# Later casts, products with v in groups of three key tiles, and the weight conversion issued ahead of the silu step

## The chip, the cores and the metric

The kernel runs on one core of a Trainium2 chip. TensorE multiplies matrices, VectorE and ScalarE do elementwise work and reductions, GpSimd (POOL in the profile) does elementwise work and issues the indirect transfers, SyncE (SP) issues the other transfers. Each engine works through its own instructions in order and waits on semaphores for the others. The metric is the device time of one execution in microseconds: 639.28 us for the kernel before, the median of 3 runs (638.69 to 642.12).

## The reference

Three stages, all in float32, on 1536 tokens (batch 2, sequence 768) of 512 features (8 heads of 64):

```python
# 1. attention among the keys whose 6 sign bits are those of the query
mask = q_bucket[:, :, :, None] == k_bucket[:, :, None, :]
scores = np.where(mask, scale * np.matmul(q, k.transpose(0, 1, 3, 2)), -1e9)
attn = softmax(scores)                      # over the 768 keys
x = np.matmul(attn, v)                      # then (tokens, 512)
# 2. dense layer with silu, 512 -> 2048 -> 512
h = x @ w_in
x = (h / (1 + np.exp(-h))) @ w_out
# 3. 8 experts, 512 -> 1024 -> 512; a token takes the expert of its largest logit,
#    and none where its skip score is not positive
y = gate * (np.maximum(xc @ w1[e], 0) @ w2[e])
out[do_compute] = xc + y
```

## The kernel before, in words

**Attention** (function `attention`, L264 to L597). Two heads make a pair; there are eight pairs (i = 0 to 7), and each has two halves of 384 queries, the units u = 0 to 15. A step is one block of 128 queries of one head: six steps per unit (`PU`), twelve per pair, 96 in all (`NS`). In the loop at L535, m is the step within the pair and pm the step within the unit. Step s issues the following, and each engine takes its part in this order:

- `em_S(s)` (L380): TensorE, four products of queries and keys into a PSUM tile S of two banks. There are two such tiles, so step s waits until the exponential of step s-2 has read its own.
- `em_T(s-2, 0)` (L409): TensorE transposes the first three of the six key tiles of P of step s-2 into a tile T (three of them); ScalarE copies them to PT.
- the casts of `PRE` for the next pair, on ScalarE: `kh` (keys) and `qa` (queries), once per head.
- `em_PV` (L426) in every second step: the products with v for two key tiles and two heads. They belong to the unit before. A unit has six key tiles, k = 0 to 5, so three such steps.
- `em_soft(s)` (L394): VectorE's row maximum mx and a small operation bs, then ScalarE's exponential into P.
- `em_T(s-2, 1)`: the other three key tiles; VectorE copies them (in the last pair ScalarE).
- `em_rc` and `em_r` (L434, L438): reciprocals of the row sums on VectorE, a transpose rT on TensorE, a copy r on ScalarE, a transfer to DRAM (r_d), and two transfers back (rb) that wait for the first. `em_out` copies the finished products; `em_x` multiplies and splits them on GpSimd.
- the operations of `POST` for the next pair: `k2` and `qb` are transfers by SP that copy a cast half to the other partitions, `kl` and `ql` are subtractions on GpSimd. Then the mask rows (`prep_rows`), loads, and at the end of the step the hook, which during pairs 2 to 5 and at the end also issues pieces of the first weight conversions.

For pair 0, which prepares pair 1, a second list of `PRE` and `POST` is used, with other step numbers.

**The silu layer** (L600 to L669, loop at L859). There are 3 blocks of 512 tokens and 16 slices f of 128 hidden features, 48 steps n. Products use a float32r high part and a remainder (hi and lo). A step multiplies (`em_h(n)`: 12 matmuls into ph on TensorE; then silu g and its cast gh on ScalarE, and the remainder gl = g - gh on VectorE, L625 to L627), then `em_out(n-1)` does the 12 matmuls o with the step before's gh, gh and gl. In the first block the weights still have to be converted from 64-bit words (`convert`, L197): for f of 4 to 15 step n = f - 2 runs `convert(f)`. Its first part (two ScalarE scalings u, L214, and two VectorE shifts, L215) is issued inside the split of the weights of step n+1 (ScalarE's whi, L249, VectorE's wlo, L252); its second part (two VectorE operations at L219, two at L223 which give wraw, then two loads of later words by SP) is issued by `for _ in cv: pass`. Weights of 512 KB halves are staged in three buffers. In the second and third block the converted weights are used again.

**The experts** follow from L916 on and are not touched.

The lines that the change touches are L528 to L533 (the lists), L551 to L553 (the products with v), L566 (the step in which r is made) and L870 to L874:

```python
if n < N:
    if n >= len(EARLY_H):
        em_h(n)
    for _ in cv:
        pass
```

Of the kernel before, what the change touches and what calls it, by code (L numbers as in the profile page):

```python
# [25 lines left out]
def kernel(  # L26
# [16 lines left out]
    nc = tc.nc  # L43
# [190 lines left out]
    def split(i):  # L234
        assert next(splitting(i), "end") == "end"
# [28 lines left out]
    def attention(hook):  # L264
# [26 lines left out]
        def prep_alloc(i):  # L291
            pl = mainp if i % 2 else evp
            ops[i] = [pl.tile([P, 2, S], F32R, name=n, bufs=1) for n in ("Q1", "K1", "Q2")] + [K2s[i % 2]]
            mks[i] = (topp.tile([P, HQ], F32, name="ma"), topp.tile([P, HQ], F32R, name="mb"))
# [78 lines left out]
        units = [(i, qh) for i in range(B * NP) for qh in range(2)]  # L373
# [6 lines left out]
        def em_S(s, parts=(0, 1)):  # L380
            u, qt, hd = steps[s]
            i, qh = units[u]
            Q1, K1, Q2, K2 = ops[i]
            q0 = qh * HQ + qt * P
            if 0 in parts:
                st_S[s] = psS.tile([P, 2, 512], F32, tag="S", name="S", bufs=2)
            ps = st_S[s]
            for j in parts:
                q_, k_, n, first = ((Q1, K1, P, True), (Q2, K2, NK2, False))[j]
                for c in range(2):  # L390
                    nc.tensor.matmul(ps[:, c, 0:HQ], q_[0:n, hd, q0:q0 + P], k_[0:n, hd, c * HQ:(c + 1) * HQ],  # L391
                                     start=first, stop=not first)
# [33 lines left out]
        def em_PV(u, k):  # L426
            i, qh = units[u]
            if k == 0:
                st_pv[u] = psTV.tile([P, HQ], F32, tag="V", name="pv", bufs=1)
            for hd in range(2):  # L430
                nc.tensor.matmul(st_pv[u][hd * D:(hd + 1) * D], vts[i][:, k, hd], st_PT[u][:, hd, k],  # L431
                                 start=(k == 0), stop=(k == KT - 1))
# [45 lines left out]
        def em_busy(n):  # L478

            for _ in range(n):  # L480
                nc.tensor.matmul(bs, busy[:, 0:P], busy, start=True, stop=True)
# [21 lines left out]
        for j, ps in enumerate(direct):  # L503
# [6 lines left out]
            else:  # L510
# [14 lines left out]
        prep_op(1, 0, "scale", nc.scalar)  # L525
        nc.gpsimd.memset(K2s[1][D:D + 32].bitcast(F32), 0.0)

        PRE = [(1, 0, "kh", nc.scalar), (3, 0, "qa", nc.scalar), (5, 1, "kh", nc.scalar), (7, 1, "qa", nc.scalar)]  # L528

        POST = [(1, 0, "k2", None), (2, 0, "kl", nc.gpsimd), (3, 0, "qb", None), (4, 0, "ql", nc.gpsimd),  # L530
                (5, 1, "k2", None), (7, 1, "kl", nc.gpsimd), (7, 1, "qb", None), (9, 1, "ql", nc.gpsimd)]

        PRE, POST = ([ops_, [(x + 2, *op) for x, *op in ops_]] for ops_ in (PRE, POST))  # L533
        rbs, xs = {}, {}
        for s in range(NS + PU + 4):  # L535
            i, m = divmod(s, 2 * PU)
            nxt = i + 1 < B * NP
            if nxt and m == 0:
                prep_alloc(i + 1)
            if s < NS:  # L540
                em_S(s, (0, 1) if s else (1,))
            if 0 <= s - 2 < NS:
                em_T(s - 2, 0)
            for mm, *op in PRE[i == 0]:
                if nxt and mm == m:
                    prep_op(i + 1, *op)
            w, pm = divmod(s, PU)
            u, k = (w - 1, pm - 2) if pm >= 2 else (w - 2, pm + 4)
            pv = 0 <= u < len(units)

            if pv and k % 2:  # L551
                em_PV(u, k - 1)
                em_PV(u, k)  # L553
            if s < NS:
                em_soft(s)
            if s == 1:
                prep_op(0, 1, "k2", nc.scalar)
                prep_op(0, 1, "kl", nc.vector)
            if s < 2:
                em_busy(2)  # L560
            if 0 <= s - 2 < NS:
                em_T(s - 2, 1)
            if pv:
                if k == 0:
                    em_rc(u)
                if k == 1:  # L566
                    rbs[u] = em_r(u)
                if k == KT - 1:
                    xs[u] = em_out(u)
                if k == 3 and u:  # L570
                    em_x(u - 1, xs.pop(u - 1), rbs.pop(u - 1), nc.gpsimd)
            if nxt:
                if m == (1 if i else 5):
                    prep_proj(i + 1)
                if m == (2 if i else 6):
                    prep_mask(i + 1, nc.gpsimd if i else nc.scalar)
                for mm, *op in POST[i == 0]:
                    if mm == m:
                        prep_op(i + 1, *op)
                if m == (4 if i else 8):  # L580
                    prep_rows(i + 1)
                if m == 0 and i + 2 < B * NP:
                    prep_load(i + 2)
                if m == (9 if i else 11) and i + 2 < B * NP:
                    prep_op(i + 2, 0, "scale", nc.scalar)
                if m == 11 and i + 2 < B * NP:
                    load_v(i + 2)
                if m == 11 and i + 2 == B * NP:
                    top_st.close()
            if s == NS - 2 * PU:  # L590
                ev_st.close()
            hook(s - NS)
            if s == NS - 1:
                psS_st.close()
# [246 lines left out]
    with tc.manual_schedule():  # L841
# [17 lines left out]
        for n in range(N + 1):  # L859
            cv = convert(n + 2) if NEARLY <= n + 2 < NF else iter(())  # L860
            while cnt["spl"] < min(n + (3 if n >= NF else 2), N):

                sp = splitting(cnt["spl"], apart=True)
                next(sp)
                next(cv, None)
                next(sp, None)
            if n >= N - 2:
                while cnt["spl"] < NM + (1 if n == N - 2 else 3) and any(h[1] > 1 for h in homes):
                    split(cnt["spl"])
            if n < N:  # L870
                if n >= len(EARLY_H):
                    em_h(n)
                for _ in cv:
                    pass  # L874
            if n == NF - 2:
                pools["stg_st"].close()
                pools["gwb"], gwb_st = opened("gwb", side="right")
                pools["gwb_t"] = pools["gwb"].tile([P, NE + 1, DM], F32, name="gwb")
                nc.sync.dma_start(pools["gwb_t"].rearrange("p c d -> p (c d)"), gr.to_broadcast([P, (NE + 1) * DM]))
            if n == 3:  # L880
                cf = pools["xo"].tile([P, DM], F32, tag="x", name="cf", bufs=6)
                nc.sync.dma_start(cf[:, 0:consts.shape[1] - NC - P], consts[:, NC + P:])
            if n == 6:
                nc.vector.tensor_copy(cb, cf[:, 0:consts.shape[1] - NC - P])
            if n == 1:
                nc.sync.dma_start(tk, tok)
                nc.gpsimd.memset(gwc, 0.0)
                nc.sync.dma_start(gwc[:, :, 0:NE + 1], gw.rearrange("(k p) c -> p k c", p=P))
                z = pools["gwb0"] = sm.tile([P, NE * NTOK // P], F32, name="zid", bufs=1)
                nc.gpsimd.memset(z, float(DUMMY))  # L890
                nc.sync.dma_start(id_d.rearrange("(p r) c -> p (r c)", p=P), z)
                zx = sm.tile([P, DM // P], F32, name="zx", bufs=1)
                nc.gpsimd.memset(zx, 0.0)
                nc.sync.dma_start(x_d[NTOK:NTOK + 1].rearrange("o (p c) -> (o p) c", p=P), zx)
                nc.sync.dma_start(g_d[NTOK:NTOK + 1], zx[0:1, 0:1])
            if n >= 1:
                em_out(n - 1)
                b, f = items[n - 1]
                if f == NF - 1 and b + 1 < len(TILES):
                    todo.extend((t, c) for t in range(*TILES[b]) for c in range(NE + 1))  # L900
            if routing is not None and next(routing, "end") == "end":
                routing = None
            if n % NF:
                for j in range(4):
                    if todo:
                        logit(*todo.pop(0))
                        if not todo:
                            bb = n // NF - 1
                            if idx is None:
                                idx = ps_tile("idx", [P, 3], "O4")  # L910
                            routing = route(*TILES[bb], L[:, TILES[bb][0]:TILES[bb][1]], ps_tile("pr", [P, 512], "X"), idx)
# [49 lines left out]
        for t in range(t1 - t0):  # L961
            x = pools["xo"].tile([P, DM], F32, tag="x", name="x", bufs=6) if t < 2 else ep.tile([P, DM], F32, tag="eo", name="x")
# [280 lines left out]
```

## Time and profile before

| | |
|---|---|
| runs of the kernel before | 639.28 us median (638.69 to 642.12, n = 3) |
| the profiled execution | 640.85 us, of which the span 639.0 us |
| TensorE matmul busy | 610.4 us (96%) |
| VectorE busy | 468.9 us (73%) |
| ScalarE busy | 403.8 us (63%) |
| GpSimd busy | 171.0 us (27%) |
| chain of waits that ended last | TensorE 74%, ScalarE 9%, VectorE 7%, issue 4%, transfers 3% |

The profile is of one execution. "Busy" counts the time in which an engine executes; matmuls are pipelined, so a busy TensorE is not one at its peak. The chain of waits is followed back from the last instruction, at each step to what released it or to the instruction before it on its engine: what stands in it set the end. Attention takes about the first 235 us, the silu layer goes to about 517, the experts from about 544 to the end.

### The profile page before, as it was taken

The page shows a single profiled execution, that of the slowest core. Times are in us where ns is not written, and L with a number is a line of the kernel's source. Part 1 is how long each engine was busy: PE and PEld are TensorE (multiplying, and loading weights), DVE is VectorE, ACT ScalarE, POOL GpSimd, SP SyncE. Part 2 cuts the span into 40 slices and gives each one's busy share as a digit, 9 for nine tenths or more (in the row PEclk, how much of TensorE's full clock was granted, in tenths as well). Part 3 has the DMA queues.
Part 4 walks back from the last instruction along what each step waited for, and adds up shares of the span by engine and source line. Part 5 has one row for each costly group of instructions (what it writes and reads, how often), then busy time and mean ns, then how long its engine had stood idle before and what let it go on. Part 6 is the DMA issues. An engine that isn't in the chain of part 4 may idle for free.

```text
span 639.0 us, 9525 instructions
## 1 busy us (share of the span) xinstructions
PE 610.4 (96%) x3239; PEld 461.9 (72%) x3239; DVE 468.9 (73%) x861; ACT 403.8 (63%) x675; POOL 171.0 (27%) x261
## 2 busy tenths in 40 slices
PE   8899999999999999998899999999999988999996
PEld 3667676666767756776678888788887766788885
DVE  6867778788787665778776777447775568899992
ACT  6978788787887984454555333444433456788881
POOL 4437556383744142000000000020000035523201
PEclk9999999999999999999999999999999999999998
DMA  3532542534224124545443000007223258999920
GB/s 109 148 120 64 173 108 82 157 74 129 65 57 105 78 78 114 176 162 168 151 146 148 0 1 2 0 3 197 90 80 128 66 132 224 363 406 406 408 78 27
DMA packets 30978, 83.45 MB, mean 131 GB/s; under 512 B 6032, under 2 KB 9810, under 8 KB 30798
## 3 DMA queue, kind: packets, MB, share of 16 engines
q1 hardware_dynamic: 28834, 79.06, 38.5%
q0 software_dynamic: 1936, 3.65, 1.7%
q8 instruction: 26, 0.43, 0.3%
q14 instruction: 26, 0.21, 0.1%
q10 hardware_dynamic: 156, 0.10, 0.1%
HBM read 67.65 MB, written 8.50 MB: 119 GB/s over the span
## 4 chain that ended last, share of the span: by engine, by line
PE 74%; ACT 9%; DVE 7%; issue 4%; DMA 3%; POOL 1%; SPq 1%; POOLq 0%; DVEq 0%; ACTq 0%
PE ph L619 17%; PE o L662 10%; PE S L391 9%; PE pv L431 9%; PE T L417 8%; PE o L653 7%; PE eh L1059 5%; PE ey L1081 5%; ACT P L405 3%; ACT u L214 2%; DVE mag L219 2%; DVE mx L401 1%; PE tr L1037 1%; DVE wraw L223 1%; ACT K L317 1%
## 5 line engine op out<-in xcount | busy, mean ns | idle before, releaser
L249 ACT CAST whi<-wraw 128x1024 fp32r<-128x1024 f32 x100 | 102.7, 1050 | 45.0 <-DVE wraw L223 38.1
L252 DVE TENSOR_TENSOR wlo<-wraw,whi 128x1024 fp32r<-128x1024 f32 x100 | 119.6, 1222 | 11.5 <-ACT whi L249 10.5
L405 ACT ACTIVATE P<-S,bs 128x768 f32<-128x768 f32 x96 | 95.5, 994 | 26.0 <-DVE bs L403 23.2
L401 DVE TENSOR_REDUCE mx<-S 128x1 f32<-128x768 f32 x96 | 91.1, 949 | 14.2 <-PE S L391 11.8
L391 PE MATMUL S<-K,Q 88*128 88x384 f32 (+1 forms) x384 | 92.5, 362 | 7.8 <-ACT P L405 6.0
L625 ACT ACTIVATE g<-ph 128x512 f32<-128x512 f32 x48 | 28.5, 595 | 107.1 <-PE ph L619 93.7
L417 PEld LDWEIGHTS T<-ident,P 128*128 128x128 f32 x576 | 68.0, 140 | 30.9 <-ACT PT L420 18.6
L627 DVE TENSOR_TENSOR gl<-g,gh 128x512 fp32r<-128x512 f32 x48 | 33.3, 693 | 77.0 <-ACT gh L626 77.0
L417 PE MATMUL T<-ident,P 128*128 128x128 f32 x576 | 88.7, 277 | 0.2 <-ACT PT L420 0.2
L791 POOL DMA_INDIRECT id_d<-tk,slot x12 | 12.1, 1006 | 261.6 <-DVE pre L799 258.5
L391 PEld LDWEIGHTS S<-K,Q 88*128 88x128 f32 (+1 forms) x384 | 63.0, 191 | 16.0 <-ACT P L405 8.8
L431 PE MATMUL pv<-PT,v 128*64 128x384 f32 x384 | 72.5, 499 | 0.0
L422 DVE COPY PT<-T 128x384 f32<-128x384 f32 x85 | 47.0, 553 | 22.0 <-PE T L417 21.3
L619 PE MATMUL ph<-xhi,whi 128*128 128x512 f32 x192 | 54.4, 405 | 6.4 <-ACT whi L249 6.4
L420 ACT COPY PT<-T 128x384 f32<-128x384 f32 x107 | 50.6, 479 | 9.4 <-PE T L417 8.7
L619 PE MATMUL ph<-xlo,whi 128*128 128x512 f32 x192 | 52.3, 394 | 0.0
L619 PE MATMUL ph<-xhi,wlo 128*128 128x512 f32 x192 | 52.1, 393 | 0.0
L619 PEld LDWEIGHTS ph<-xhi,whi 128*128 128x128 f32 x192 | 34.6, 188 | 17.8 <-ACT whi L249 10.6
L675 DVE CUSTOM_DVE_ANT_0 junk<-x,gwb 128x512 bf16<-128x512 f32 x72 | 45.4, 686 | 0.0
L619 PEld LDWEIGHTS ph<-xlo,whi 128*128 128x128 f32 x192 | 36.1, 188 | 8.5
L619 PEld LDWEIGHTS ph<-xhi,wlo 128*128 128x128 f32 x192 | 36.1, 188 | 8.3
L431 PEld LDWEIGHTS pv<-PT,v 128*64 128x64 f32 x384 | 23.3, 136 | 25.5 <-issue 25.2
(177 smaller groups left out, 1049.9 us busy)
## 6 DMA issues: line engine op xcount, KB each, us to landing
wraw<-in_w_dram SPq DMA_DIRECT2D x64, 512.0 KB
w<-in_mw_dram SPq DMA_DIRECT2D x32, 512.0 KB
v<-in_vt_dram SPq DMA_DIRECT2D x8, 384.0 KB
rb<-r_d SPq DMA_DIRECT2D x32, 96.0 KB
out_dram<-x SPq DMA_DIRECT2D x12, 256.0 KB
x_d<-x SPq DMA_DIRECT2D x11, 256.0 KB
raw<-in_kT_dram SPq DMA_DIRECT2D x7, 384.0 KB
raw<-in_qT_dram SPq DMA_DIRECT2D x7, 384.0 KB
```

What stands on the lines that cost most here:

```text
L249: nc.scalar.copy(hi[:, sl], t[:, sl])
L252: eng.tensor_tensor(lo[:, sl], t[:, sl], hi[:, sl].bitcast(F32), op=ALU.subtract)
L391: nc.tensor.matmul(ps[:, c, 0:HQ], q_[0:n, hd, q0:q0 + P], k_[0:n, hd, c * HQ:(c + 1) * HQ], start=first, stop=not first)
L401: nc.vector.tensor_reduce(mx[:, 0:1], ps[:, :, 0:HQ], axis=AX.XY, op=ALU.max, negate=True)
L405: nc.scalar.activation(pt.rearrange("p (a b) -> p a b", a=2), ps[:, :, 0:HQ], AF.Exp, bias=bs_[:, 0:1], scale=bs_[:, 1:2], accum_out=st_su ...
L417: nc.tensor.transpose(ps[:, j], pt[:, k * P:(k + 1) * P], ident)
L420: nc.scalar.copy(dst, ps)
L422: nc.vector.tensor_copy(dst, ps)
L431: nc.tensor.matmul(st_pv[u][hd * D:(hd + 1) * D], vts[i][:, k, hd], st_PT[u][:, hd, k], start=(k == 0), stop=(k == KT - 1))
L619: nc.tensor.matmul(p_[:, 0:c1 - c0], w[:, k * P:(k + 1) * P], x[:, k, t0 * P + c0:t0 * P + c1], start=(q == 0), stop=(q == len(ops3) - 1))
L662: nc.tensor.matmul(acc[t], g[:, (t - t0) * P:(t - t0 + 1) * P], w[:, DM:PIECE], start=(f == 0 and q == 0), stop=(f == NF - 1 and q == 2))
L675: nc.vector.tensor_tensor_reduce(junk, xts[t], pools["gwb_t"][:, c], op0=ALU.mult, op1=ALU.add, scale=1.0, scalar=0.0, accum_out=L[:, t, c ...
```

## The change

There are four edits.

1. The casts and copies for head 1 of the next pair are issued in later steps (for pairs 1 and later): casts in 7 and 9 rather than 5 and 7, the transfers k2 and qb in 7 and 9 rather than 5 and 7, the subtractions in 8 and 10 rather than 7 and 9. In pair 0 all of them get other numbers: casts in 2, 4, 6, 8 (before: 3, 5, 7, 9), k2 and qb in 2, 4, 6, 8 (before: 3, 5, 7, 9), kl and ql in 3, 5, 7, 9 (before: 4, 6, 9, 11).
2. The products with v are issued for three key tiles in every third step rather than for two in every second.
3. For the last unit r is made at k = 3 rather than at k = 1.
4. In the silu layer the second part of the conversion is issued before em_h(n) rather than after it.

```diff
-        PRE = [(1, 0, "kh", nc.scalar), (3, 0, "qa", nc.scalar), (5, 1, "kh", nc.scalar), (7, 1, "qa", nc.scalar)]
+        PRE = [(1, 0, "kh", nc.scalar), (3, 0, "qa", nc.scalar), (7, 1, "kh", nc.scalar), (9, 1, "qa", nc.scalar)]
         POST = [(1, 0, "k2", None), (2, 0, "kl", nc.gpsimd), (3, 0, "qb", None), (4, 0, "ql", nc.gpsimd),
-                (5, 1, "k2", None), (7, 1, "kl", nc.gpsimd), (7, 1, "qb", None), (9, 1, "ql", nc.gpsimd)]
-        PRE, POST = ([ops_, [(x + 2, *op) for x, *op in ops_]] for ops_ in (PRE, POST))
+                (7, 1, "k2", None), (8, 1, "kl", nc.gpsimd), (9, 1, "qb", None), (10, 1, "ql", nc.gpsimd)]
+        PRE, POST = ([ops_, [(x + (1 if x < 5 else -1), *op) for x, *op in ops_]] for ops_ in (PRE, POST))
...
-            if pv and k % 2:
+            if pv and k % 3 == 2:
+                em_PV(u, k - 2)
                 em_PV(u, k - 1)
                 em_PV(u, k)
...
-                if k == 1:
+                if k == (1 if u + 1 < len(units) else 3):
                     rbs[u] = em_r(u)
...
             if n < N:
+                for _ in cv:
+                    pass
                 if n >= len(EARLY_H):
                     em_h(n)
-                for _ in cv:
-                    pass
```

## Rows read from the trace of the kernel before

**Rows 1.** Busy time by stretch: PE, PEld, DVE, ACT, POOL, clock, DMA share, GB/s

```profile
270.00:329.70 59.70, 53.38 (x222) 40.58 (x220) 45.46 (x74) 30.65 (x47) 0.00 (x0) 1.00 0.41 135
```

**Rows 2.** Chain of waits (start us, us, what), first block of the silu layer

```profile
284.18 1.24 ACT u L214 x2
...
286.60 0.69 DVE gl L627
...
290.69 1.23 ACT u L214 x2
```

**Rows 3.** Chain of waits, second block of the silu layer

```profile
352.11 2.80 PE ph L619 x12
354.91 2.76 PE o L662 x12
```

**Rows 4.** Timeline (start, us, engine, line, idle before), one step of the first block

```profile
284.31 1.23 DVE L252 TENSOR_TENSOR wlo<-wraw,whi 128x1024 fp32r<-128x1024 f32 x1 [0.22 <-ACT whi L249]
...
287.21 1.29 DVE L219 SCALAR_TENSOR_TENSOR mag<-u,mag 128x512 int32<-128x512 int32 x2
...
288.41 1.29 DVE L223 SCALAR_TENSOR_TENSOR wraw<-u,mag 128x512 int32<-128x512 int32 x2
...
289.62 0.76 DVE L215 TENSOR_SCALAR mag<-w 128x512 int32<-128x512 int32 x2
289.73 1.05 ACT L249 CAST whi<-wraw 128x1024 fp32r<-128x1024 f32 x1 [3.17 <-DVE wraw L223]
```

**Rows 5.** Chain of waits, attention of the last pair of heads

```profile
194.29 1.44 PE pv L431 x8
195.73 0.48 PE T L417 x3
196.21 0.70 PE S L391 x4
196.91 0.66 PE T L417 x6
```

**Rows 6.** Chain of waits, step 3 of pairs 1 and 7, and a projection

```profile
45.90 1.44 PE pv L431 x8
...
69.94 0.78 PE pj L338 x8
...
211.64 1.44 PE pv L431 x8
```

**Rows 7.** Timeline of attention, single instructions

```profile
26.01 0.98 PE L391 MATMUL S<-K,Q 128*128 128x384 f32 x4 [0.78 <-ACT P L405]
...
39.34 0.94 PE L391 MATMUL S<-K,Q 128*128 128x384 f32 x4 [1.47 <-DMA Q<-Q]
...
107.64 0.84 ACT L317 ACTIVATE K<-raw 64x768 fp32r<-64x768 f32 x1
...
117.69 0.24 ACT L444 COPY r<-rT 6x128 f32<-6x128 f32 x1
...
119.20 1.11 SPq L448 DMA_DIRECT2D rb<-r_d  x2
...
239.85 0.27 PE L442 MATMUL rT<-ident,sums 128*6 128x128 f32 x1 [1.00 <-DVE sums L436]
```

**Rows 8.** Chain of waits, from S to the end of its exponential

```profile
226.95 0.72 PE S L391 x4
...
227.69 0.97 DVE mx L401
...
228.68 0.17 DVE bs L403
...
228.94 1.08 ACT P L405 x2
```

**Rows 9.** The page's groups of instructions: ScalarE's copies of transposed tiles

```profile
L420 ACT COPY PT<-T 128x384 f32<-128x384 f32 x107 | 50.6, 479 | 9.4 <-PE T L417 8.7
```

**Rows 10.** Chain of waits, the transfer that copies Q for pair 1

```profile
36.12 3.08 DMA Q<-Q
```

## The prediction

> **What bounds the kernel now.** I cut the span into stretches first. From 270 to 329.7 us TensorE is busy for 53.4 of 59.7 us, at the full clock [rows 1]: something else paces it there. The chain of waits of that stretch repeats the same pieces every 6.51 us (ScalarE's u at 284.18 and 290.69), and between them stands VectorE's gl [rows 2]. Further on, a step of the silu layer is only its twelve ph and twelve o matmuls, 2.80 + 2.76 = 5.56 us [rows 3]. So the stretch is paced by the weight conversion, and TensorE could go some 0.95 us faster per step. The timeline says why: whi waits 3.17 us for wraw (L223), and wraw comes only after gl, which itself waits for silu and its cast [rows 2, 4].
>
> Attention is bound by TensorE, but barely. The chain of its last pair of heads is nothing but TensorE: pv 1.44, T 0.48 behind it (0.15 more than half of the 0.66 of six T elsewhere), S 0.70, T 0.66, S 0.70, T 0.33 [rows 5]. That is 4.31 us for a heavy step and a light one. From pv at 45.90 to pv at 211.64 the chain passes six times through twelve steps in 165.74 us [rows 6]. TensorE alone would need 6 x 6 x 4.31, five projections at about 0.98 (pj 0.78 [rows 6] and a slower S behind it) and twelve rT at some 0.1 (0.27 recorded, beside its neighbours [rows 7]) = 161.3 us; the other 4.4 us are waits, as where a cast of 0.84 us [rows 7] sits ahead of an exponential.
>
> A second number decides what follows: the loop that returns an S buffer. There are two, so S of step s+2 waits for the exponential of step s. In the chain this runs S 0.72, mx 0.97, bs 0.17, P 1.08 with small gaps, from 226.95 to 230.02, 3.07 us, and some 0.04 more until S may start [rows 8]: 3.11. A heavy and a light step take 4.31, so the loop is hidden now. Two light steps in a row take 2 x 1.36 = 2.72: it would not be. The trace has such a place, at the start, where no pv runs yet: S of step 8 waits 0.78 us for P, and, having stopped, takes 0.98 rather than 0.70 [rows 7].
>
> **Part 1, conversion ahead of the silu step.** em_h issues on TensorE, ScalarE and VectorE; what is left of cv issues on VectorE, then two DMAs on SP. So only VectorE's order changes: per step shift, wlo, L219, L223, then gl, rather than gl in front of L219. By the rows this is 0.76 + 1.23 + 1.29 + 1.29 + 0.69 = 5.26 us [rows 2, 4], and while ScalarE makes whi (1.05) VectorE has gl and shift to do (1.45). So VectorE is 0.3 us faster than TensorE's 5.56. What is now late is gl, by the 2.6 us of the two pairs ahead of it. Its reader is the last third of o, and TensorE reaches that a whole ph of the next step and two thirds of o (2.80 + 1.84) after the silu step's own ph has ended. As VectorE is the faster engine it runs ahead until the conversion for the step after next is done before gh is there; then gl follows gh at once, as today. The gain is the 59.7 us of the stretch over 6.51, nine steps, at 0.95 us: **-8.5 us**. Ends: 0, if the 512 KB halves of w, of which three buffers exist, can't come every 2.8 us; and -8.5. The trace shows no wait on them; I take -8.5. Later stretches move forward as a block, and their loads are triggered by the kernel itself.
>
> **Part 2, products with v in threes.** Per unit six key tiles now take two heavy steps, not three. A heavy step is 0.70 + 0.33 + 12 x 0.18 + 0.48 = 3.67 us, so a triple is 2 x 1.36 + 3.67 = 6.39; by pairs, 6.47. TensorE saves 0.08 us per triple, the switch. Against this stands the loop: in every triple the heavy step's S follows two light ones. It may start 3.11 us after the first light one, not 2.72, and costs 0.98 instead of 0.70: 0.39 + 0.28 = 0.67 us lost. pv stands behind that S and behind T of the same step in the queue, so it can't fill the hole; T needs the same P. rT (0.11) falls into it. A triple becomes 7.06. Six times twelve steps: 24 x 7.06 + 5 x 0.98 = 174.3, against 165.74: **+8.6 us**, although all of today's 4.4 us of waits are taken as gone. Ends: -6.2 (no loop at all: 24 x 6.39 + 12 x 0.1 + 4.9 = 159.5) and +18 (a wait of 0.78, as at the start, for 0.39 in each); the chain's loop is of the same pairs of heads, so I take its 0.39. The last pair adds three loops, 3 x (0.67 - 0.08) = **+1.8**.
>
> On the restart the trace shows 0.28 us [rows 7]. The Trainium skill, "TensorE: Matmul & The Clock Gate", section "Single matmul latency", puts a matmul that cannot hide its drain at about 166 ns over one in a stream. By that estimate a triple would lose 0.11 us less and the whole 2.6 us less. The measured row stays in the sum.
>
> **Part 3, casts and copies in later steps.** For pairs 1 to 6 kh and qa of head 1 go to steps 7 and 9, kl and ql to 8 and 10, the DMAs k2 and qb to 7 and 9. Casts then never stand in the first light step of a triple (2, 5, 8, 11), whose exponential is the critical one; a heavy step has room for one. That is what lets today's waits go. But qb, SP's DMA of Q into the other half, goes from step 7, where nothing is ahead of it, to step 9, behind the r_d and rb DMAs of em_r, and rb waits until r_d has landed. Step by step, from S of step 8: its P ends at 3.4 us; then on ScalarE a T copy 0.48 [rows 9], the cast 0.84, P of step 9 1.09, r 0.24: 6.05. From r's end to rb's issue 1.27 (117.93 to 119.20), rb 1.11, then Q at 8.5 [rows 7]. The one Q transfer that the chain shows took 3.08 us [rows 10]: it lands at 11.6, S sees it at 11.7. Step 13 (head 1 of the next pair) would start 3.40 + 3.70 + 3.40 = 10.5 after S of step 8. So it comes 1.2 us late at worst; with the 1.27 of the small r_d instead, not late at all. The row of the same transfer is nearer, but v and raw loads were issued right behind it: I take 0.8, six times: **+4.8** (0 to +7.2). The same transfer by the Trainium skill, "DMA: Bandwidth & Descriptors", section "Anatomy of one DMA", is 2.0 us plus bytes over 436 GB/s, an estimate of 2.45 us: then 0.6 late each time, 3.4 in all.
>
> For pair 1 the same DMA goes the other way, from step 9, behind r_d, to step 8, ahead of it. Today S of step 13 waits 1.47 us for it [rows 7, 10]: **-1.4** (0 to -2.5; the mask rows then leave later). In pairs 2 to 5 the shift of an early conversion in step 4 (half of the 0.76 [rows 4]) now stands ahead of the mx of a first light step: 0 to 1.6 together, **+1.0**.
>
> **Part 4, r of the last unit one pv group later.** rT waits 1.00 us for sums today [rows 7]; the third tile's pv (0.72) fills most of that, rT stays where it is, and one switch less and one tile more follow: **-0.5**. If rb came late, POOL's last x and the second silu step behind it would lose about as much.
>
> **Sum.** -8.5 + 8.6 + 1.8 + 4.8 - 1.4 + 1.0 - 0.5 = +5.8 us. The profiled execution took 640.85 us (span 639.0 and 1.85 around it), 1.57 above the median of 639.28; it would be 646.7, and the median 645.1.
>
> **Rivals.** Each is the sum with one term replaced.
> (a) The loop is covered, so the change is faster. Place: S of the heavy step. For it: the chain of attention is TensorE almost throughout. Against it: the loop of 3.11 and the wait at 26.01 [rows 7, 8]. It decides as soon as S two steps apart may start within 2.72 us. Then -8.5 - 6.2 - 0.2 - 1.4 - 0.5 = -16.8: 622.4 us.
> (b) Q arrives in time: the 4.8 falls away, 640.3 us, no change. For it: a 3 KB transfer takes 1.27. Against: 3.08 [rows 10].
> (c) The conversion gains nothing, because w is late: the 8.5 falls away, 653.6. For it: only three half buffers; against: no wait on w in the chain.
>
> **Chances.** Forecast 0.50 (its own range 641 to 650), (a) 0.22, (b) 0.18, (c) 0.10. The range 628 to 653 leaves out most of (a) and half of (c). About 0.5%, 3.2 us, is what a measurement here can tell from no change. Slower by more: forecast but its lowest part 0.46, and (c) 0.10: 0.56. Within: (b) and the rest, 0.22. Faster: 0.22.
>
> **What would show it.** After the change the period of u should be 5.5, with no whi wait of TensorE (part 1); pv groups in attention at 7.1 us with S waiting for P once per triple (part 2; 6.4 would be (a)); S of head 1's first step waiting for the Q DMA once per pair (part 3); no such wait at 39 us. The forecast is wrong if attention ends before 235 us.

## The result, and the profile after

The changed kernel takes 650.08 us (median of four, 649.35 to 650.59), the kernel before, beside it, 638.99. The recorded ratio is 1.0143, with a 95% interval of [1.0111, 1.0174]; the two medians alone give 1.0174. Forecast were 645.1 us and slower. The profiled execution took 650.59 us (span 648.8), 9.74 more than the one of before; the sum forecast 5.8 for that difference. The repeats of before spread over 637 to 642.4 us in the experiments below, which is why the intervals are some 0.3% wide to each side. One of e3's ten executions below took 1201.49 us, and without it e3's median is 640.90 rather than 641.73.

Stage by stage, by the ends of instructions in the two traces: the last product with v ends at 264.70 us, before at 245.95, so attention is 18.8 us longer. The silu layer returns 8.7 of these, and the experts differ by 0.2. Both halves of the forecast show in this; attention is the part that was worse than forecast. But 1.3 us of the 18.8 are not the change's: the exponential of step 1, ahead of which no line is edited, starts that much later in this execution. The chains of waits have it in the kernel before, and then in the after kernel:

```profile
14.34 1.08 ACT P L405 x2
```

```profile
15.67 1.08 ACT P L405 x2
```

So attention is 17.4 us longer from there on, and the sum's 5.8 stands against 8.4.

**Conversion.** The windows of the after kernel (columns as in [rows 1]), and the chain of waits in the same block:

```profile
270.00:320.00 50.00, 50.00 (x216) 40.33 (x216) 46.21 (x76) 32.12 (x48) 2.20 (x7) 1.00 0.61 199
```

```profile
284.61 2.80 PE ph L620 x12
287.40 2.76 PE o L663 x12
290.17 2.73 PE ph L620 x12
```

TensorE is busy all the time, and the chain is TensorE alone: 5.56 us from ph to ph, where [rows 2] had ScalarE's u every 6.51. The timeline of the after kernel shows the new order on VectorE:

```profile
284.23 1.28 DVE L219 SCALAR_TENSOR_TENSOR mag<-u,mag 128x512 int32<-128x512 int32 x2
285.44 1.28 DVE L223 SCALAR_TENSOR_TENSOR wraw<-u,mag 128x512 int32<-128x512 int32 x2
286.64 0.68 DVE L628 TENSOR_TENSOR gl<-g,gh 128x512 fp32r<-128x512 f32 x1
286.75 1.05 ACT L249 CAST whi<-wraw 128x1024 fp32r<-128x1024 f32 x1 [1.42 <-DVE wraw L223]
```

gl now stands behind L219 and L223. whi still waits 1.42 us for wraw, against 3.17 in [rows 4], but no matmul waits for whi any more (before, ph did, ten times and 6.4 us in all).

**Attention.** TensorE's timeline of the after kernel, one pair of heads (start, us, engine, line; in brackets the idle time before it and what ended it):

```profile
84.01 0.97 PE L391 MATMUL S<-K,Q 128*128 128x384 f32 x4 [0.56 <-ACT P L405]
85.25 2.16 PE L431 MATMUL pv<-PT,v 128*64 128x384 f32 x12
90.76 0.27 PE L442 MATMUL rT<-ident,sums 128*6 128x128 f32 x1 [0.17 <-DVE sums L436]
92.30 2.16 PE L431 MATMUL pv<-PT,v 128*64 128x384 f32 x12
99.07 0.94 PE L391 MATMUL S<-K,Q 128*128 128x384 f32 x4 [1.41 <-DMA Q<-Q]
100.27 2.16 PE L431 MATMUL pv<-PT,v 128*64 128x384 f32 x12
106.86 0.27 PE L442 MATMUL rT<-ident,sums 128*6 128x128 f32 x1 [0.25 <-DVE sums L436]
108.29 2.16 PE L431 MATMUL pv<-PT,v 128*64 128x384 f32 x12
114.22 0.97 PE L391 MATMUL S<-K,Q 128*128 128x384 f32 x4 [0.58 <-ACT P L405]
```

Groups of pv start 7.05, 7.97, 8.02 and 7.15 us apart (the next one at 115.44): a triple is 7.05; with the late Q it is 0.9 more, and with the next pair's projection 1.0 more. In front of every group stands a hole, with another name each time: S waits for P, or rT for sums (which VectorE makes after mx and bs), or S for Q. Where no rT and no Q stands in the way, the chain of the after kernel goes round the loop as forecast:

```profile
204.26 0.97 DVE mx L401
...
205.33 0.17 DVE bs L403
...
205.58 1.09 ACT P L405 x2
...
206.72 0.96 PE S L391 x4
...
208.01 2.09 PE pv L431 x12
```

With S of 0.72 at 203.52 in front, that is the loop of [rows 8], now between two S of TensorE: 3.20 us from S to S instead of 2.72, and the late S takes 0.96 rather than 0.72. The three largest waits of TensorE from 28 to 262 us, by cause (us in total, times, longest); three smaller ones make 3.6 us:

```profile
PE S L391 <- DMA Q<-Q: 9.1, 6, 1.7
PE S L391 <- ACT P L405: 4.5, 9, 0.6
PE rT L442 <- DVE sums L436: 2.7, 12, 0.4
```

SP's queue in the same kernel, ahead of the next late Q:

```profile
123.45 0.24 ACT L444 COPY r<-rT 6x128 f32<-6x128 f32 x1
123.72 0.29 SPq L445 DMA_DIRECT2D r_d<-r  x1
124.97 1.13 SPq L448 DMA_DIRECT2D rb<-r_d  x2
126.15 0.59 SPq L314 DMA_DIRECT2D Q<-Q  x1
```

rb is issued 1.28 us after the end of r, and Q 1.18 after that (1.27 and 1.11 in the working). From S of step 8, at 117.83, Q's issue is 8.3 us away, where 8.5 was worked out. Then the chain of waits has the transfer itself, which answers to [rows 10]:

```profile
126.15 3.04 DMA Q<-Q
```

S starts behind it, at 129.32.

### The profile page after: what moved, and what is told of

Same layout as the page of the kernel before. It is cut to its first block, busy times and chain, and to the rows that moved or that the text cites. A ratio compares the mean times of both kernels' runs of the same rounds, so it can differ in the third digit from the quotient of the medians.

```text
span 648.8 us, 9542 instructions
## 1 busy us (share of the span) xinstructions
PE 613.1 (94%) x3239; PEld 465.0 (72%) x3239; DVE 467.3 (72%) x861; ACT 404.8 (62%) x675; POOL 173.8 (27%) x261
## 4 chain that ended last, share of the span: by engine, by line
PE 72%; DVE 9%; ACT 6%; issue 5%; DMA 4%; POOL 3%; SPq 1%; POOLq 0%; DVEq 0%; ACTq 0%
PE ph L620 21%; PE o L663 14%; PE pv L431 7%; PE o L654 7%; PE eh L1061 6%; PE ey L1083 5%; PE S L391 5%; DVE mx L401 4%; ACT P L405 3%; DMA Q<-Q 3%; PE T L417 3%; POOL Q L330 2%; POOL K L325 1%; DVE PT L422 1%; PE tr L1039 1%
## 5 line engine op out<-in xcount | busy, mean ns | idle before, releaser
L417 PE MATMUL T<-ident,P 128*128 128x128 f32 x576 | 85.7, 276 | 1.3 <-ACT PT L420 1.3
L431 PE MATMUL pv<-PT,v 128*64 128x384 f32 x384 | 70.3, 502 | 0.0
L431 PEld LDWEIGHTS pv<-PT,v 128*64 128x64 f32 x384 | 25.1, 138 | 29.7 <-issue 29.7
L330 POOL TENSOR_TENSOR Q<-raw,Q 64x192 fp32r<-64x192 f32 x64 | 37.2, 610 | 27.8 <-ACT Q L320 27.3
```

What stands on the lines that cost most here:

```text
L330: eng.tensor_tensor(Q2[0:D, hd, c], qs[r, c], Q1[r, hd, c].bitcast(F32), op=ALU.subtract)
L417: nc.tensor.transpose(ps[:, j], pt[:, k * P:(k + 1) * P], ident)
```

## Experiments

| kernel | edits | median us | ratio [95%] |
|---|---|---|---|
| after | 1, 2, 3, 4 | 650.08 | 1.0143 [1.0111, 1.0174] |
| e1_conv | 4 | 631.32 | 0.9866 [0.9814, 0.9918] |
| e2_pairs | 1, 3, 4 | 633.40 | 0.9913 [0.9873, 0.9953] |
| e3_qfirst | 1, 2, 3, 4, Q ahead of r_d | 641.73 | 1.0036 [1.0009, 1.0063] |
| e4_shortmax | 1, 2, 3, 4, short maximum | 631.92 | 0.9897 [0.9867, 0.9927] |
| e5_shortmax_before | short maximum | 636.30 | 0.9955 [0.9924, 0.9986] |
| e6_pvfirst | 1, 2, 3, 4, pv ahead of S | 646.18 | 1.0082 [1.0051, 1.0113] |
| e7_triples | 2 | 660.81 | 1.0332 [1.0288, 1.0375] |
| e9_pairs_qfirst | 1, 3, 4, Q ahead of r_d | 625.80 | 0.9788 [0.9756, 0.9821] |

**The conversion alone** (edit 4 on the kernel before):

```diff
+                for _ in cv:
+                    pass
                 if n >= len(EARLY_H):
                     em_h(n)
-                for _ in cv:
-                    pass
```

> The kernel before with edit 4 alone: the rest of the conversion is issued ahead of the silu step. My theory (VectorE's order set the pace of the first block, and TensorE's own 5.5 us takes over): 8.8 us faster than before, 630.2 us, u every 5.5 us, and no wait of TensorE for whi. Rival (the gain in the changed kernel came from the delay that attention had already suffered, which gave the loads time): the period stays near 6.5 us and the time within 2 us of 639.

It took 631.32, 7.9 less than before beside it (639.17). In its first block TensorE is busy for 55.00 of 55.00 us (255 to 310 us). The conversion's gain is shown, and w is not late.

**The change with pv in pairs** (edits 1, 3 and 4):

```diff
-            if pv and k % 3 == 2:
-                em_PV(u, k - 2)
+            if pv and k % 2:
                 em_PV(u, k - 1)
                 em_PV(u, k)
```

> The changed kernel with the products with v again for two key tiles in every second step (edit 2 undone; the later casts, the later last r and the conversion stay). Theory (two light steps in a row expose the loop S, mx, bs, P, S): S no longer waits once per triple, twelve steps take 28.0 rather than 30.2 us although the transfer of Q for head 1 still comes late, and the time is 630 us, between 627 and 633. Rival (the later casts and the late transfer of Q carry the loss): 644 to 650.

It took 633.4, just above the range that was expected: the triples cost 650.08 - 633.4 = 16.7 us. S waits for P only twice (0.4 us in all), and twelve steps take 28.4 to 29.3 us. In steps from the kernel before it is -7.9 for the conversion, 633.4 - 631.3 = +2.1 for the other two edits with pairs (no more than the two intervals leave open), and +16.7 for the triples. That the three add up is no check, as each step starts where the one before it ends. The repeats lie in groups, at 629.3 to 629.5, 632.4 to 633.4 and 637.5 to 637.9; the mean granted clock is 0.993 in all four of the last group and 0.996 to 0.999 in the others. The profiled execution (637.91) is of the last group. Its timeline, and its windows behind that row:

```profile
68.34 1.62 PE L391 MATMUL S<-K,Q 128*128 128x384 f32 x4 [2.83 <-DMA Q<-Q]
```

```profile
68.00:70.00 2.00, 1.66 (x6) 1.59 (x7) 0.00 (x1) 0.00 (x0) 0.00 (x0) 0.50 0.97 324
72.00:74.00 2.00, 2.00 (x9) 0.61 (x5) 0.00 (x0) 1.31 (x3) 0.00 (x0) 0.50 1.00 385
```

S waited 2.83 us for Q here, and behind that wait TensorE ran at a granted clock of 0.50 (1.2 GHz) until 75 us: S took 1.62 instead of 0.94. Q was held up by r_d: rb was issued 3.0 us after it this time (60.92 and 63.94), not 1.25.

**Q ahead of r_d and rb on SP**, everything else as in the change:

```diff
+            for mm, *op in POST[i == 0]:
+                if nxt and mm == m and op[1] == "qb":
+                    prep_op(i + 1, *op)
             if pv:
                 if k == 0:
                     em_rc(u)
...
                 for mm, *op in POST[i == 0]:
-                    if mm == m:
+                    if mm == m and op[1] != "qb":
                         prep_op(i + 1, *op)
```

> The changed kernel with the transfer qb issued ahead of the r_d and rb transfers of the same step. Theory (Q lands late because it stands behind r_d on SP): S of step 13 starts 3.4 us after S of step 11, as in the other triples, not 4.4; six times 1.0 us, and 1.6 us of slow clock behind the longest wait go as well: 643 us. Rival (Q waits for its own cast, or the r_d chain then comes late and holds the unit's end): within 2 us of 650.

It took 641.73, 8.3 us less than the change. No S waits for Q any more, and TensorE's mean clock is 0.997 or more in every execution (0.991 to 0.998 in the change). But S of the same step is still late, by half: it starts 3.90 us after the S two steps earlier, where the other triples have some 3.42 and 4.43 what it was with Q late. (These are starts in the timeline, which draws a queued S from some 0.24 us earlier; in the chain of waits the loop is 3.20.) The timeline of this kernel shows it:

```profile
122.29 0.94 PE L391 MATMUL S<-K,Q 128*128 128x384 f32 x4
124.30 1.14 POOL L468 TENSOR_TENSOR xlo<-x,xhi 128x192 fp32r<-128x192 f32 x2
124.33 0.58 DVE L403 SCALAR_TENSOR_TENSOR bs<-mx 128x2 f32<-128x2 f32 x1
125.01 0.99 ACT L405 ACTIVATE P<-S,bs 128x768 f32<-128x768 f32 x1 [0.93 <-DVE bs L403]
126.19 0.95 PE L391 MATMUL S<-K,Q 128*128 128x384 f32 x4 [0.94 <-POOL xlo L468]
```

The releaser named is GpSimd's xlo, but that ended at 125.44. P, with the read of its row sums behind it (125.90, 0.19 us), ends at 126.09, right before S. So it is the loop again, with a bs of 0.58 us instead of 0.16.

Over the six pairs this S is late by 2.4 us here and by 6.4 in the change, so Q itself cost 4.0, and 1.3 more by the clock (below). The traces agree: from S of step 2 to the end of the last product with v it is 243.4 us here and 249.0 in the change, 5.6 less. The rest of the 8.3 is not shown to be the queue's; 1.4 us between the profiled executions lie ahead of S of step 2 (14.31 and 15.68).

**A short maximum**, on the change (e4) and as a control on the kernel before (e5): the row maximum is taken over the first 96 scores, so mx is shorter (0.26 us for 0.96) and the loop with it; the rest of the work is the same, though the softmax is not.

```diff
-nc.vector.tensor_reduce(mx[:, 0:1], ps[:, :, 0:HQ], axis=AX.XY, op=ALU.max, negate=True)
+nc.vector.tensor_reduce(mx[:, 0:1], ps[:, 0:1, 0:96], axis=AX.XY, op=ALU.max, negate=True)
```

> The changed kernel with the row maximum taken over the first 96 of the 768 scores only, so that for a part of the queries the softmax is another one. mx should fall from 0.96 to about 0.25 us and the loop from 3.43 to about 2.7, TensorE's own time for two light steps. Theory: the wait of S for P vanishes in all triples (27 times 0.65 us), of which the later Q transfer, now relatively later, takes back some 3 to 4: about 636 us. Rival (the light steps are slow for a reason of TensorE's own, loads of weights or transposes): 648 us or more.

> The kernel before with the row maximum over the first 96 of 768 scores only, so that for a part of the queries the softmax is another one: the control of the same cut in the changed kernel. There the cut gave 18 us. If it did so through the exposed loop, it gives little here, where a window holds 4.3 us: at most the 4.4 us of waits that attention has, 635 to 638 us. Rival (VectorE's time itself was the limit in both): 621 to 625 us.

On the change it gave 18.2 us (650.08 to 631.92), more than expected; on the kernel before 2.3 (638.58 to 636.30). The loop thus costs the change some 16 us that it does not cost the kernel before. The chain of waits of e4 shows what is left when the loop fits:

```profile
42.80 2.09 PE pv L431 x12
...
49.24 2.08 PE pv L431 x12
```

6.44 us from group to group (6.39 in the working, without rT), nothing but TensorE in between. S of head 1's first step still waits for Q, 1.35 to 1.64 us, six times.

**pv ahead of S** in the step that has it, so that the products stand in front of the late S and could fill its hole:

```diff
+            if pv and k % 3 == 2:
+                em_PV(u, k - 2)
+                em_PV(u, k - 1)
+                em_PV(u, k)
             if s < NS:
                 em_S(s, (0, 1) if s else (1,))
```

(u, k and pv are worked out above it; the call in its old place is gone.)

> The changed kernel with the products with v issued ahead of S in their step, not behind it. Theory of the window (in a cycle of three steps a single burst lies in two of the three windows from S to S two steps on, so one window is always 2.7 us and shorter than the loop of 3.4): the wait of S for P moves to another step of the triple and the time stays within 3 us of 650. Rival (only the order in the queue is at fault; what can run ahead of the waiting S fills the hole): 27 times 0.67 less, 632 us.

It took 646.18, 3.9 us less than the change and a little more than the 3 us allowed for. No S waits for Q in it. The hole has moved, not gone, as its chain of waits shows:

```profile
108.10 0.90 PE S L391 x4
...
109.03 0.97 DVE mx L401
...
110.09 0.37 DVE bs L403
...
110.55 1.09 ACT P L405 x2
...
111.69 0.97 PE S L391 x4
...
113.31 2.09 PE pv L431 x12
```

S at 111.69 now belongs to the light step ahead of the burst, and S waits for P in it 10.6 us in all (16 times). Three steps with one burst in them have three spans from S to the S two steps on; two hold the burst, one does not, wherever it is put.

**Triples alone** (edit 2 on the kernel before):

> The kernel before with edit 2 alone: three key tiles in every third step, the casts where they were. Theory: the loop costs 27 times 0.67 us less the 0.08 saved per group, as in the changed kernel, and the cast in step 5, which is now a first light step, stands in the loop and adds up to 0.5 us per pair; Q is not late. About 655 us. Rival (the three edits of attention only cost together): 640 us or less.

It took 660.81, 22.2 us more than before and more than expected. Two places, from its timeline:

```profile
114.05 0.84 ACT L317 ACTIVATE K<-raw 64x768 fp32r<-64x768 f32 x1
114.92 0.99 ACT L405 ACTIVATE P<-S,bs 128x768 f32<-128x768 f32 x1
...
116.06 0.97 PE L391 MATMUL S<-K,Q 128*128 128x384 f32 x4 [0.85 <-ACT P L405]
...
258.23 0.27 PE L442 MATMUL rT<-ident,sums 128*6 128x128 f32 x1 [2.53 <-DVE sums L436]
258.43 3.85 PE L431 MATMUL pv<-PT,v 128*64 128x384 f32 x12
```

With the old step numbers a cast stands ahead of the critical exponential, and in the last unit rT waits 2.53 us for sums, after which a group of pv takes 3.85 us instead of 2.16. From the third last group of pv to the end of the last it is 17.0 us, in the after kernel, with edit 3, 13.0. So edits 1 and 3 do serve the triples; they don't pay for them.

**Without triples, with Q first** (edits 1, 3 and 4, and Q ahead of r_d):

> Edits 1, 3 and 4 of the change without edit 2 (products with v for two key tiles in every second step), and the transfer qb issued ahead of r_d and rb. If the two causes found so far add up, nothing in attention waits for more than a few tenths: twelve steps 27.3 to 27.6 us, against 28.0 before; no long wait for Q and so no stretch at the lower clock; 627 us, 4 less than the conversion edit alone. Rival (the later casts bring nothing by themselves, because the waits only move): 631 us, as the conversion edit alone.

It took 625.80, 0.9788 times the kernel before [0.9756, 0.9821], and less than any other kernel here.

With it four kernels, all with edits 1, 3 and 4, make a square: triples with Q late 650.08 and with Q first 641.73, pairs with Q late 633.40 and with Q first 625.80. By these medians the triples cost 16.7 us with Q late and 15.9 with Q first, and the late Q 8.3 with triples and 7.6 with pairs, so the two causes add up. The same window of attention in this kernel, and in the after kernel:

```profile
28.00:262.00 234.00, 233.22 (x1444) 164.27 (x1443) 182.95 (x346) 186.24 (x372) 113.20 (x187) 1.00 0.37 108
```

```profile
28.00:262.00 234.00, 213.70 (x1350) 148.59 (x1348) 166.28 (x322) 176.71 (x357) 108.50 (x183) 0.99 0.31 91
```

TensorE is busy for 233.22 of 234 us, against 213.70 (TensorE's is the second column).

## Why the prediction was right, and where its sizes were off

**Part 1** held: 8.7 us between the traces and 7.9 alone, for 8.5. VectorE runs ahead, as worked out: at 286.64 us gl starts 1.3 after gh has ended, and at 316.38 it waits for gh.

**Part 2** held by its mechanism and its price. A triple was to take 7.06 us and takes 7.05; without the loop 6.39 was worked out and 6.44 measured. That 7.05 meets 7.06 so closely is in part luck: the loop took 3.20 for 3.11, against which the late S took 0.96 for 0.98 and the twelve pv 2.09 for 2.16. Rival (a) is excluded: the loop is in the open. The working had one place for it, S waiting for P once per triple. Only nine waits bear that name; at two of four groups in a pair rT waits for sums instead, and at one S waits for Q. With a short maximum one wait for P (0.6 us) and one for sums (0.4) are left, so the common part ahead of both, mx and the steps behind it, is what is late.
The restart was taken as 0.28 us. It is 0.24 to 0.25 (0.96 or 0.97 against 0.72).
The 166 ns that the Trainium skill gives for it ("TensorE: Matmul & The Clock Gate", section "Single matmul latency"), for a single bf16 matmul, was too small for this chain of four.
Counted to the start of its third last group of pv, the last pair lost 3.1 us rather than 1.8, and the tail from there on gained 0.3 rather than 0.5 (part 4).

**Part 3** had the right place and too small a price; this is the step that was mis-sized. Forecast were 0.8 us for each late Q, 4.8 in all and at most 7.2. Measured by the S two steps earlier, S is late by 1.04, 0.96, 1.01, 0.91, 1.27 and 1.20 us in the six pairs, 6.4 in all. In the chain of waits the six transfers take 3.08, 3.00, 3.04, 2.94, 3.31 and 3.23 us: the lateness is the transfer less 2.03 or 2.04, each time. The working had this sum, with 3.08 from [rows 10], and got 1.2; the 0.8 lay between that and the nothing that the 1.27 of the small r_d would give, and the row of the same transfer was the one to take. (The 2.45 us worked out from the Trainium skill, "DMA: Bandwidth & Descriptors", section "Anatomy of one DMA", were too few in each; that section is on transfers issued by GpSimd, and SP issues Q.) What the working left out is that 2.4 of the 6.4 us would be lost without a late Q too, by the slow bs that e3 shows. The 1.27 came with the longest transfer, and behind it the clock fell, which no term had. Windows of the after kernel:

```profile
188.00:190.00 2.00, 0.28 (x3) 0.07 (x2) 1.90 (x4) 1.45 (x3) 0.47 (x1) 1.00 0.96 234
191.00:192.00 1.00, 1.00 (x5) 0.51 (x5) 0.96 (x1) 0.68 (x3) 0.00 (x0) 0.50 0.00 0
195.00:196.00 1.00, 1.00 (x13) 0.40 (x11) 0.48 (x1) 0.48 (x1) 0.00 (x0) 1.00 0.01 0
```

After the wait of 1.72 us for Q that ended at 190.01 the granted clock was 0.50 from 191 to 194, and the pv group there took 3.39 us instead of 2.09. From S at 190.01 to the same S of the next pair, at 222.01, it is 32.00 us; the three stretches from 68.85 to 159.48 are 30.21 each on the mean (forecast 30.0). Rival (b), Q in time, is excluded.
Of the two small terms, the wait of 1.47 us of today fell away, as forecast: S of step 13 starts 0.6 us earlier (38.72 for 39.34) although this execution was 1.3 late at step 1, so the start gained 1.9 for 1.4. The shift ahead of mx in step 4 costs 0.1 per pair, not 0.25.

**What the triples cost in all.** The forecast booked the vanished waits of before (4.4 us) with the triples. Put with the casts, its terms read: triples 24 x (7.06 - 6.47) = 14.2, less 1.2 for the rT that falls into the hole, and 1.8 for the last pair, 14.8; casts -4.4 + 4.8 - 1.4 + 1.0 = 0. Measured are 16.7 and, with the small edit 3, +2.1. With Q first the casts are worth 625.8 - 631.3 = -5.5 (the two intervals overlap by a little), where the same terms without the 4.8 give -4.8. So the two ideas of the change that move work, casts into later steps and the conversion ahead of silu, were both good. The sum failed on the triples, and on a queue that Q was moved behind.

Of the 5.0 us from 645.1 to 650.1, 1.3 are the late start of the profiled execution. They have one more part: the sum gave the difference 5.8 us, and the profiled executions differ by 9.74; by the medians it is 11.1, since the profiled execution of before lay 1.9 us above the median of its four runs and that of after 0.5.

**Left open.** Nothing separates the share of the loop in rT's waits from that in S's. The low clock in the slowest group of e2's repeats was seen in one trace only. The other groups of repeats may come from the start: in the profiled executions of e4, e5 and e9 the first matmuls on the keys and queries (pd, six) take 2.2 to 2.5 us and S starts at 7 us, in the other seven they take 4.0 and S starts at 9.2 or 9.3, with a listed clock of 1.00 in both. Why is open, and for it differences of some 2 us between medians are not safe. A third S buffer, which might hide the loop without shortening it, was not tried.

## What to carry to other kernels

When buffers are returned by a loop over other engines, compare the loop with the shortest stretch of the schedule between two uses, not with its mean: grouping into bursts kept the mean (6.47 us for three steps, then 6.39) and shortened that stretch from 4.31 to 2.72, below the loop of 3.2. Order inside the period does not end the hole, as e6 shows; a shorter loop (e4) or an even spread (e2, e9) does. And when a transfer is moved to a later step, look at what waits at the head of its queue there: behind an issue that waits for another transfer to land, Q cost 6 us by the traces and 8 by the medians, and one reordering took them back.

## What the runs showed of the hardware

**TensorE's clock fell behind single waits.** The granted clock went to 0.50 (1.2 GHz) after waits of 1.72 us (change), 2.83 (e2) and 2.53 (e7), for some 3 to 7 us; after the change's other waits for Q, 1.37 to 1.65 us, S took its usual 0.93 to 0.95. The price comes on top of the wait: 1.3 us for one pv group. What decides it is not settled by these few.

**A tiny VectorE operation can take more than three times as long beside GpSimd.** bs takes 0.16 us, and 0.58 where it starts 0.03 after GpSimd's xlo (rows of e3). xlo is two instructions, 1.14 us together, and bs ends about when the first of them must have. The Trainium skill, "SBUF — State Buffer", section "SBUF: two separate sides", says that VectorE with two SBUF inputs and GpSimd lock a shared pair of ports for a whole instruction; bs reads mx twice, and the row agrees. In a loop with no slack these 0.4 us are on the path.
